# Layer 2's Wo on packed rows, one uncast Q/K product, quarter loads of x, and instruction orders as lists

## Chip, cores and metric

The kernel runs on one core of one Trainium2 chip. The metric is device time of one execution in microseconds (us). The core has TensorE (PE, with its weight loads shown apart as PEld), VectorE (DVE), ScalarE (ACT), GpSimd (POOL) and SyncE (SP). SP computes nothing here; it issues most DMAs, one after the other in the order of its list, and so is a queue of its own.

## The reference

Four layers run in turn on x of 2048 tokens by 448 features: attention (A), gated product (B), A, B, with the same weights each time. Every layer normalises its input and adds its result to x.

```python
x = A_x
x = x + _A_ref(_layernorm(x, axis=-1), A_wqkv, A_wo)
x = x + _B_ref(_layernorm(x, axis=-1), B_w_gate, B_w_up, B_w_down)
x = x + _A_ref(_layernorm(x, axis=-1), A_wqkv, A_wo)
x = x + _B_ref(_layernorm(x, axis=-1), B_w_gate, B_w_up, B_w_down)
```

A has 16 heads of 28 features. A token attends to itself and the seven tokens 2, 4, ... 14 back; the heads' outputs go through Wo (448 by 448). B computes (x Wgate) * (x Wup) with 1792 features, then Wdown.

## The kernel before

All of x and all weights stay on chip. The kernel calls the layers 0 to 3; layers 0 and 2 are A, layers 1 and 3 are B. A layer is cut into four chunks of 512 tokens, and `SEQ` (line 230) interleaves chunks of neighbouring layers: A00 A01 B10 A02 B11 and so on, where B12 is layer 1, chunk 2.

**Units.** `ln_chunk` (743) normalises four blocks of 128 tokens: statistics on DVE (`bn_stats`, 751), a logarithm and an exponential on ACT that give rstd (754, 756), the normalisation on DVE (772) and a transpose, either on PE with an eviction (781, 787) for the chunks that `PE_T` (30) names, or by a DMA that SP issues (775). `qk_chunk` (838) makes Q and K of a chunk in four units, each with a K and a Q half that run at the same time on the two halves of PE's 128 rows; a unit is two parts (`crossed`, 795), the second of which starts once the first has left PE. Evictions go to `qk` (872). `v_group` (887) makes V for a group of one or two query blocks of 120 tokens; there are 9 groups, g0 to g8. `attn_front` (940) makes logits (958), exponentials (970) and masks them (979); `attn_back` (1003) multiplies by V (997), sums, inverts on ACT (1026, 1027) and writes normalised heads to `oT` (1047). In layer 2 the logits of one group and the V product of the group before are one PE unit (`pe_joint`, 931). `y_blocks` (1052) does the Wo product for two neighbouring blocks of tokens, and `x_block` (1064) adds it to x. `b_chunk` (1075) makes 14 gate/up units of 128 features (1095), evicts (1101) and multiplies (1104) them, then runs the down product in four parts for each of two pairs of blocks (834).

**Padding.** In `oT` and `wo_g` a head has 32 rows, 28 of them used: four heads in 128 rows, four such chunks c for 16 heads. The Wo product of two blocks goes through these four chunks for each half of the rows, in two "flips", one for each pairing of row halves with blocks: 16 matmuls of 64 rows and 448 columns. The last four of 32 rows hold zeros in `wo_g`. Q and K of chunks 2 and 3 and of layer 2 already use such spare rows, filled by DMAs from `qk` to `qk` (878); chunks 0 and 1 of layer 0 (`FULLQ`) do not.

**Start.** SP and ACT load x's chunk 0 in two halves, then V's weights, then the Q/K weights into `stage`, which is the not yet used `hT`. ACT, DVE and GpSimd cast them into `WQK` with 32 rows for a head (lines 695 to 706, priority -28), 12 copies, and all Q/K units wait for all of them (`WQKR`). PE runs warm-up matmuls (692) until data is there. Gate/up weights are loaded in 14 steps, each behind the one before (713 to 716).

**Order.** `Sched` lays all units out before the program is emitted: it keeps a clock for every engine and takes the ready unit with the best priority. `TUNE` shifts priorities of single units by number. The outcome is one fixed list for each engine, which the engine runs strictly in order, waiting on semaphores where a unit's inputs come from elsewhere.

Of the kernel before, what the change touches and what calls it, by code (L numbers as in the profile page):

```python
# [29 lines left out]
PE_T = ("00","01","02")  # L30
# [8 lines left out]
POOL_MASK = 1  # L39
WQK_ENGS = ("act", "dve", "pool")  # L40
FULLQ = ("00", "01")
LN0 = (2,2)
# [4 lines left out]
TUNE = {  # L47
# [185 lines left out]
def qb_info(qb):  # L233

    if qb == 0:
        return 0, 128, 0, 128
    tok = 128 + QB * (qb - 1)
    return tok - 8, 128, tok, QB


STRADDLE = next(q for q in range(NQB) if qb_info(q)[2] < HALF < qb_info(q)[2] + qb_info(q)[3])
assert qb_info(STRADDLE)[0] + KW == HALF


def group_span(g):

# [30 lines left out]
class Sched:  # L277
# [34 lines left out]
    def finish_of(self, key):  # L312
        op, n = self.ready[key]
        if op.dma is not None:
            return max(o.end + o.lat for o in self.dgroup[(op.dma, op.mode)])
# [260 lines left out]
def build(nc, A_x, A_wqkv, A_wo, B_w_gate, B_w_up, B_w_down, out):  # L576
# [46 lines left out]
    def one(fn, key=None):  # L623
        return [(fn, key)]
# [630 lines left out]
```

## Time and profile before

| what | us |
|---|---|
| three runs | 395.64, 395.96, 396.29 |
| profiled execution, its own time | 395.34 |
| span of its profile | 393.5 |
| PE busy | 383.4 |
| DVE busy | 268.7 |
| ACT busy | 182.8 |

The granted clock is 1.00 in all stretches. The span begins with GpSimd's first constant and ends with the last store. PE's busy share contains 48 warm-up matmuls (8.9 us). Rows of the chain of waits show a start, a length and an engine with its line; "issue" is time in which the profile shows nothing that the engine waited for. Rows of stretches show start and end, length, busy time of each engine, the granted clock, the DMA share and GB/s.

### The profile page before, as it was taken

Reading aid. Unit: us, or ns where it says so; the run is one execution under the profiler, and the core shown is the slowest. Engines: PE = TensorE matmul, PEld = TensorE weight load, DVE = VectorE, ACT = ScalarE, POOL = GpSimd, SP = SyncE. Lnnn points to the kernel's source line nnn. Section 1 sums busy time; section 2 is a strip of 40 time slices with the busy share of each in tenths; the row PEclk is TensorE's granted clock in tenths of the full one; section 3 lists DMA queues with packets and bytes.
Section 4 is the critical chain, followed back from the end, with each engine's and each line's share of the span. In section 5 each row is a group of like instructions: output and inputs, shape, how many; then the busy total and the mean of one; then the engine's idle time right before and its main releaser. Section 6 shows DMA issues by size and latency. Waiting matters only on the chain.

```text
span 393.5 us, 12725 instructions
## 1 busy us (share of the span) xinstructions
PE 383.4 (97%) x5678; PEld 208.5 (53%) x5678; DVE 268.7 (68%) x577; ACT 182.8 (46%) x297; POOL 8.9 (2%) x29
## 2 busy tenths in 40 slices
PE   8999978999999999999999989999999999999997
PEld 6545544445545454455445545577545555544555
DVE  5996999997996375367874678843689893244323
ACT  4788775554536442464334543333646442134110
POOL 6110000000000000000000000000000000000000
DMA  8645473524230072000330002510003204100002
GB/s 273 189 91 132 109 110 105 85 49 50 48 42 15 13 97 55 2 13 4 66 68 16 16 3 50 72 28 13 27 26 72 27 2 93 45 5 2 23 2 72
DMA packets 50766, 21.74 MB, mean 55 GB/s; under 512 B 41912, under 2 KB 49816, under 8 KB 50712
## 3 DMA queue, kind: packets, MB, share of 16 engines
q1 hardware_dynamic: 49720, 19.95, 25.5%
q8 instruction: 45, 0.74, 0.8%
q10 hardware_dynamic: 992, 0.98, 0.7%
q14 instruction: 9, 0.07, 0.1%
HBM read 8.43 MB, written 1.84 MB: 26 GB/s over the span
## 4 chain that ended last, share of the span: by engine, by line
PE 92%; DVE 3%; DMA 2%; issue 1%; ACT 1%; ACTq 0%
PE ps L1095 43%; PE ps L834 26%; PE ps L818 16%; PE ps L958 2%; PE ps L997 2%; PE ps L1116 1%; DMA hT<-in_A_wqkv_dram 1%; DMA xnTb<-xn_sb 1%; DVE xn_sb L772 1%; DVE hT L1104 1%; ACT g_sb L1101 0%; ACTq L631 0%; DVE E_sb L979 0%; PE ps L781 0%; DVE qk L872 0%
## 5 line engine op out<-in xcount | busy, mean ns | idle before, releaser
L1095 PE MATMUL ps<-xnTb,WGU 64*128 64x512 bf16 x1568 | 178.4, 376 | 1.2 <-DMA xnTb<-xn_sb 0.9
L1095 PEld LDWEIGHTS ps<-xnTb,WGU 64*128 64x128 bf16 x1568 | 85.1, 94 | 84.5 <-issue 6.1
L1101 ACT ACTIVATE g_sb<-ps 128x512 bf16<-128x512 f32 x112 | 66.0, 596 | 110.2 <-PE ps L1095 86.4
L1104 DVE TENSOR_TENSOR hT<-g_sb,ps 128x512 bf16<-128x512 bf16 x112 | 75.8, 683 | 53.6 <-ACT g_sb L1101 50.6
L834 PE MATMUL ps<-WD,hT 64*128 64x448 bf16 x840 | 85.5, 349 | 0.1
L834 PEld LDWEIGHTS ps<-WD,hT 64*128 64x128 bf16 x840 | 43.9, 94 | 35.5 <-DVE hT L1104 0.6
L1065 DVE TENSOR_TENSOR x_sb<-x_sb,ps 128x448 bf16<-128x448 bf16 x62 | 35.8, 614 | 26.2 <-PE ps L834 26.2
L818 PE MATMUL ps<-xnTa,WQK 64*128 64x512 bf16 (+1 forms) x448 | 47.7, 356 | 0.0
L970 ACT ACTIVATE E_sb<-ps 128x1024 bf16<-128x1024 f32 (+1 forms) x36 | 33.6, 977 | 14.3 <-PE ps L958 13.9
L772 DVE TENSOR_SCALAR xn_sb<-x_sb,mv,rstd 128x512 bf16<-128x512 bf16 (+1 forms) x64 | 35.5, 581 | 6.2 <-ACT rstd L756 6.1
L751 DVE BATCH_NORM_STATS2 st<-x_sb 128x6 f32<-128x448 bf16 x64 | 37.4, 611 | 2.3 <-DMA x_sb<-in_A_x_dram 2.3
L818 PEld LDWEIGHTS ps<-xnTa,WQK 64*128 64x128 bf16 x448 | 23.5, 94 | 19.4 <-DVE qk L872 0.5
L834 PE MATMUL ps<-wo_g,oT 64*128 64x448 bf16 x256 | 30.5, 350 | 1.5 <-issue 1.5
L818 PE MATMUL ps<-WV,xnTa 64*128 64x448 bf16 (+1 forms) x252 | 28.5, 340 | 0.7 <-DVE hT L1104 0.4
L872 ACT ACTIVATE qk<-ps 128x1024 bf16<-128x1024 f32 (+1 forms) x23 | 21.5, 948 | 14.0 <-PE ps L818 13.9
L754 ACT ACTIVATE lnv<-mv,eps_sb 128x2 f32<-128x2 f32 x32 | 9.5, 300 | 32.7 <-DVE mv L753 32.7
L979 DVE TENSOR_TENSOR E_sb<-E_sb,MK 128x1024 bf16<-128x1024 bf16 (+2 forms) x39 | 23.2, 610 | 1.3 <-ACT E_sb L970 1.2
L1047 DVE TENSOR_TENSOR oT<-ps,R_sb 128x448 bf16<-128x448 f32 (+2 forms) x38 | 21.0, 597 | 2.8 <-ACT R_sb L1027 2.7
L1026 ACT ACTIVATE R_sb<-R_sb 128x960 f32<-128x960 f32 (+1 forms) x18 | 17.3, 961 | 11.4 <-DVE R_sb L1024 11.4
L872 DVE CAST qk<-ps 128x1024 bf16<-128x1024 f32 (+1 forms) x9 | 9.9, 1102 | 16.1 <-PE ps L818 16.1
L834 PEld LDWEIGHTS ps<-wo_g,oT 64*128 64x128 bf16 x256 | 12.6, 94 | 12.8 <-issue 1.9
L818 PEld LDWEIGHTS ps<-WV,xnTa 64*128 64x128 bf16 x252 | 12.2, 94 | 10.8 <-PE ps L818 1.6
(45 smaller groups left out, 179.2 us busy)
## 6 DMA issues: line engine op xcount, KB each, us to landing
out_dram<-x_sb SPq DMA_DIRECT2D x15, 112.0 KB, 1.7
WGU<-in_B_w_gate_dram SPq DMA_DIRECT2D x7, 224.0 KB, 3.4
WGU<-in_B_w_up_dram SPq DMA_DIRECT2D x7, 224.0 KB, 3.7
WD<-in_B_w_down_dram SPq DMA_DIRECT2D x14, 112.0 KB, 2.1
x_sb<-in_A_x_dram SPq DMA_DIRECT2D x3, 448.0 KB, 7.1
qk<-qk SPq DMA_DIRECT2D x24, 28.0 KB
xnTb<-xn_sb SPq DMA_TRANSPOSE x32, 3.1
hT<-in_A_wqkv_dram SPq DMA_DIRECT2D x2, 224.0 KB, 5.2
```

Of the source, the lines that this page charges most:

```text
L751: sc.add("dve", one(lambda E, B=B: E.bn_stats(st6[:, B, :], x_sb[:, B, :]), ("bn", li, B)), 525.0, deps=[("x", li - 1, B)] + ([("xn", li - ...
L772: sc.add("dve", one(lambda E, B=B, dst=dst, src=src: E.tensor_scalar(dst, src, mv[:, B, 0:1], rstd[:, B:B + 1], ALU.subtract, ALU.mult), ( ...
L818: parts[0 if s < 3 else 1][1].append((lambda E, w=w, c=c, lo=lo, st=st, sp_=sp_: E.matmul(u["out"](w), u["lhs"](w, c, lo, lo + 64), u["rhs ...
L834: ins.append((lambda E, w=w, c=c, lo=lo, st=st, sp_=sp_: E.matmul(outs(w), lhs(w, c, lo), rhs(w, c, lo), start=st, stop=sp_), keys[w] if s ...
L872: return E.activation(dst, src, ACT.Copy) if hasattr(E, "activation") else E.tensor_copy(dst, src)
L970: return E.activation(E_sb[:, slot, 2 * hp:2 * hp + 2, 0:w], ps[:, b0:b0 + 2, 0:w], ACT.Exp, scale=SCALE)
L979: return E.tensor_tensor(e, e, m, ALU.mult)
L1047: return E.tensor_tensor(dst, src, rec, ALU.mult)
L1065: sc.add("dve", one(lambda E: E.tensor_tensor(x_sb[:, B, :], x_sb[:, B, :], ps[:, bk[w], 0:D], ALU.add), ("x", li, B)), dve_est(D), deps=[ ...
L1095: ins.append((lambda E, u=u, k=k, w=w: E.matmul(u["out"](w), WGU[64 * w:64 * w + 64, k, 128 * u["fc"]:128 * u["fc"] + 128], X[64 * w:64 * ...
L1101: sc.add("act", one(lambda E, gs=gs, bk=bk: E.activation(g_sb[:, gs, 0:n], ps[:, bk[0], 0:n], ACT.Copy), ("G", li, jp, fc)), act_est(n), d ...
L1104: sc.add("dve", one(lambda E, gs=gs, bk=bk, fc=fc: E.tensor_tensor(hT[:, fc, hs, h0:h1], g_sb[:, gs, 0:n], ps[:, bk[1], 0:n], ALU.mult), ( ...
```

## The change

1. **Layer 2's Wo.** The 16 heads have 448 features and need only 7 half chunks of 64 rows for each block, not 8. For all chunks of layer 2 (`WX`), `move_heads` sends heads 12 to 15 of two blocks, 8 small loads for each chunk of tokens, from chunk 3 of `oT` to spare rows: two heads for one of the blocks, the other two for the other. `wo_g` gets three more slots with the other two heads' rows: a copy of slots 0 to 2 on ACT or DVE (`wo_c`) and 10 small loads behind layer 0's Wo. `y_twin` replaces `y_blocks`: it pairs blocks B and B+2 and runs 8 matmuls in the first flip and 6 in the second, and waits for all 8 loads of the chunk.
2. **One uncast Q/K product.** The first unit of layer 0, chunk 0 (`DIRECT`) reads `stage` itself: 56 matmuls of 64 rows by 32 columns of weights, four side by side for each that was, instead of 14.
3. **Weight casts** go to ACT and DVE alone, behind the normalisation of block 3.
4. **x's chunk 0** comes in four loads, two on SP and two on ACT.
5. **Transposes** of layer 0's chunk 2 go by DMA instead of PE (`PE_T`).
6. **Small moves:** zeroing `wo_g` goes from DVE to GpSimd, the mask of chunk 0 from GpSimd to DVE; some reuse waits name all readers instead of the last.
7. **Orders.** `TUNE` is empty; `ORDER` gives the list of units of every engine by number, and the clock's picture of loads and of PE's instruction loads is extended (it now only chooses PSUM banks, since the order is given).

```diff
-PE_T = ("00","01","02")
+PE_T = ("00", "01")
...
-POOL_MASK = 1
-WQK_ENGS = ("act", "dve", "pool")
+POOL_MASK = 0
+WQK_ENGS = ("act", "dve")
+WQK_P = -18.6
 FULLQ = ("00", "01")
+DIRECT = ("000",)
+BULK = "sp"
+CHAIN = True
+WX_ENG = "sp"
+WX = ("20", "21", "22", "23")
...
-TUNE = {
...
+TUNE = {}
+ORDER = {
+    "pe": [
...
+WX_MOVES = (((0, 64, 4), (2, 80, 3), (1, 96, 4), (3, 112, 3)),
+            ((2, 0, 4), (0, 16, 3), (3, 32, 4), (1, 48, 3)))
...
+                if ORDER:
+                    op = self.ops[ORDER[e][len(order[e])]] if len(order[e]) < len(ORDER[e]) else None
+                    if op is None or op not in pend[e] or self.ready_at(op, e) > now + 1e-6:
+                        continue
...
-    load_x(0, (0, 1, 2), "sp", 2400.0, -60)
-    load_x(0, (1, 2, 2), "act", 3000.0, -60)
...
+    load_x(0, (0, 1, 4), "sp", 2150.0, -60)
+    load_x(0, (1, 2, 4), "act", 2300.0, -60)
+    load_x(0, (2, 3, 4), "sp", 2170.0, -59.9)
+    load_x(0, (3, 4, 4), "act", 2400.0, -59.9)
...
-    memset("dve", wo_g[:], 0.0, "c_wo", 1000)
+    memset("pool", wo_g[:, 0:4, :], 0.0, "c_wo", 1400)
...
-            sc.add(WQK_ENGS, one(fn, ("wqk", c, w)), dict(zip(("act", "dve", "pool"), ests)), deps=[("stg", c), "c_wqk0"], prio=-28)
+            sc.add(WQK_ENGS, one(fn, ("wqk", c, w)), dict(zip(("act", "dve", "pool"), ests)), deps=[("stg", c), ("xn", 0, 3), "c_wqk0"], prio=WQK_P)
...
+        def fw(E):
+            return E.activation(wo_g[:, 4:7, :], wo_g[:, 0:3, :], ACT.Copy) if hasattr(E, "activation") else E.tensor_copy(wo_g[:, 4:7, :], wo_g[:, 0:3, :])
+        sc.add(("act", "dve"), one(fw, "wo_c"), {"act": 1350.0, "dve": 800.0}, deps=WO, prio=-17.5)
...
+                        plain_dma("sp", wo_g[pads, s:s + z - a, :], rows[:, a:z, :], ("wop", o, b, a), "d_wop", deps=plain + ["wo_c"], lat=1600.0, prio=-16.5, svc=(300.0, 700.0))
...
+                for b in range(u.get("cols", 0)):
+                    ins.append((lambda E, w=w, c=c, lo=lo, st=st, sp_=sp_, b=b: E.matmul(
+                        u["out"](w)[32 * b:32 * b + 32], u["lhs"](w, c, lo, lo + 64)[b], u["rhs"](w, c, lo, lo + 64), start=st, stop=sp_, tile_position=(lo, 32 * b)),
+                        u["keys"][w] if sp_ and b == 3 else None))
...
+            direct = f"{li}{j}{c}" in DIRECT
...
+                if direct:
+                    o = 2 * D * dc + (0 if which else D) + 4 * DH * c
+                    return [stage[lo:hi, o + DH * b:o + DH * b + 32] for b in range(4)]
...
+    def move_heads(li, j, o, prio):
+        t0 = 512 * j % HALF + 256 * o
+        B = 4 * j + 2 * o
+        nd = [("N", li, g) for g in range(NGRP) if group_span(g)[2] < 128 * (B + 2) and group_span(g)[3] > 128 * B]
+        for b, row, m in WX_MOVES[o]:
+            plain_dma(WX_ENG, oT[32 * b + DH:32 * b + 32, 0:m, t0:t0 + 256], oT[row:row + 4 * m, 3, t0:t0 + 256], ("WX", li, j, o, b), f"d_w{o}{j}", deps=nd,
+                      lat=2000.0, prio=prio - 0.3, mode=li, est=680.0 if WX_ENG == "sp" else 500.0, svc=(300.0, 700.0))
+
+    def y_twin(li, B, prio):
+        bk = Banks(2, pair=BPAIR)
+        j = B // 4
+        cols = (128 * (B % 8), 128 * ((B + 2) % 8))
+        keys = (("Y", li, B), ("Y", li, B + 2))
+        parts = []
+        for flip in (0, 1):
+            ins = []
+            for c in range(3 if flip else 4):
+                for h in (0, 1):
+                    w, lo = h ^ flip, 64 * h
+                    ins.append((lambda E, w=w, c=c, lo=lo, flip=flip: E.matmul(ps[:, bk[w], 0:D], oT[lo:lo + 64, c, cols[w]:cols[w] + 128], wo_g[lo:lo + 64, c + 4 if w and c < 3 else c, :],
+                                                                             start=flip == 0 and c == 0, stop=flip == 1 and c == 2), keys[w] if flip and c == 2 else None))
+            parts.append((flip, ins, []))
+        crossed(parts, [("WX", li, j, o, b) for o in range(2) for b in range(4)] + WOP, prio, pe_cols(D), bk)
+        for w in range(2):
+            x_block(li, B + 2 * w, bk, w, keys[w], prio)
...
+                    if f"{li}{B // 4}" not in WX:
+                        y_blocks(li, B, pr)
+                        continue
+                    move_heads(li, B // 4, B // 2 % 2, pr)
+                    if B % 4 == 2:
+                        y_twin(li, B - 2, pr)
+                        y_twin(li, B - 1, pr)
```

The numbers in `ORDER` count the calls that add a unit. Read with that count, the lists say this of the places that matter below. PE: four transposes, the two V units of g0 and g1, the uncast Q/K unit, the other three units of chunk 0, four transposes of chunk 1, the logits of g0 and g1, Q/K of chunk 1, V of g3 and g2, logits of g2, Wo of blocks 0 and 1, Q/K of chunk 2. In layer 2, between the joint unit of g3 and g2 and the first Wo part of chunk 0 there stand three gate/up units and five down parts; between the V product of g8 and the first Wo part of chunk 3 two down parts, the Wo of chunk 2 (two pairs of blocks), one gate/up unit and four down parts. ACT: the copy `wo_c` stands behind the first Q/K eviction and ahead of the second. SP: the four transposes of chunk 2 stand among gate/up loads 2 and 3.

More of the change, by code (lines that the diff above doesn't have):

```diff
@@ L261 @@
     __slots__ = ("engs", "ins", "est", "deps", "mode", "prio", "acquire", "release", "idx", "eng",
-                 "dma", "lat", "after", "start", "end", "seen", "selfd")
+                 "dma", "lat", "svc", "land", "after", "start", "end", "seen", "selfd")
     def __init__(self, **kw):
@@ L314, in finish_of @@
         if op.dma is not None:
-            return max(o.end + o.lat for o in self.dgroup[(op.dma, op.mode)])
+            return max(o.land for o in self.dgroup[(op.dma, op.mode)])
         if n == len(op.ins) - 1:
@@ L357, in pick_banks, with fetch_delay, landing @@
         return cand[:req.n]
+    def fetch_delay(self, now, est, n):
+        a, self.fetched = self.fetched, self.fetched + n
+        z, late = self.fetched, 0.0
+        k = int((a - self.NEED) // 256) + 1
+        while k >= 0 and 256 * k + self.NEED < z:
+            if k in self.arrive and 256 * k + self.NEED >= a:
+                late = max(late, self.arrive[k] - (now + late + est * (256 * k + self.NEED - a) / n))
+            k += 1
+        k = max(0, int((a - self.ASK) // 256) + 1)
+        while 256 * k + self.ASK < z:
+            if k not in self.arrive:
+                ask = now + late + est * max(0.0, 256 * k + self.ASK - a) / n
+                self.arrive[k] = max(ask + self.FETCH, self.arrive.get(k - 1, 0.0) + 1300.0)
+            k += 1
+        return late
+    def landing(self, op):
+        if op.svc is None:
+            return op.end + op.lat
+        svc, tail = op.svc
+        a = max(op.end + op.lat - tail - svc, self.moving)
+        z = a + svc
+        for k in sorted(self.arrive):
+            f1 = self.arrive[k]
+            f0 = f1 - self.FETCH_DMA
+            if f0 < z and f1 > a:
+                z += f1 - max(a, f0)
+        self.moving = z
+        return z + tail
     def schedule(self):
+        self.fetched, self.arrive, self.moving = 0, {}, 0.0
         self.ready_cache = {}
@@ L394, in schedule @@
                 best = None
+                if ORDER:
+                    op = self.ops[ORDER[e][len(order[e])]] if len(order[e]) < len(ORDER[e]) else None
+                    if op is None or op not in pend[e] or self.ready_at(op, e) > now + 1e-6:
+                        continue
+                    if op.acquire is not None and self.pick_banks(op.acquire, now) is None:
+                        continue
+                    best = op
                 cands = []
-                for op in pend[e]:
+                for op in () if ORDER else pend[e]:
                     r = self.ready_at(op, e)
@@ L460, in schedule @@
                     mode = op.mode
+                    est += self.fetch_delay(now, est, 2 * len(op.ins))
                 op.start, op.end = now, now + est
+                op.land = self.landing(op)
                 free[e] = op.end
@@ L497, in schedule @@
         self.order = order
-        self.total = max(op.end + op.lat for op in self.ops)
+        self.total = max(op.land for op in self.ops)
     def emit(self, nc, block, sems):
@@ L800, in crossed @@
                 xid[0] += 1
-                tags = [("cross", xid[0], h) for h in (0, 1)]
-                ins = ins[:-2] + [(fn, [t] + ([k] if k is not None else [])) for (fn, k), t in zip(ins[-2:], tags)]
+                tags = [("cross", xid[0], h) for h in range(2 * cols)]
+                ins = ins[:-2 * cols] + [(fn, [t] + ([k] if k is not None else [])) for (fn, k), t in zip(ins[-2 * cols:], tags)]
                 nextk = tags
@@ L861, in rhs @@
                 return X[lo:hi, dc, t0:t0 + n]
[L862 removed]
+            return dict(bk=bk, out=out, lhs=lhs, rhs=rhs, n=n, deps=[("stg", k) for k in range(4)] + ["c_stg"] if direct else WQKR, keys=(("Kps", li, j, c), ("Qps", li, j, c)), c=c, **({"cols": 4} if direct else {}))
         us = [unit(c) for c in range(4)]
```

106 lines of the change are left out of this document (66 added, 40 removed), and 226 rows, old and new, of tables (ORDER, TUNE).

## The prediction

> **What bounds the kernel now.** I read the page first, then the chain of work that ended last, then busy times by stretch, then single tiles. The page has TensorE at 97% of the span; the second row is the instruction queue, used below.
>
> ```profile
> PE 383.4 (97%) x5678; PEld 208.5 (53%) x5678; DVE 268.7 (68%) x577; ACT 182.8 (46%) x297; POOL 8.9 (2%) x29
> ...
> q8 instruction: 45, 0.74, 0.8%
> ```
>
> That share counts warm-up matmuls too, so I cut the span where the first real product starts (about 11.2 us) and where the first gate/up product starts (60.8 us). In the busy times by stretch the first number is the length, then PE, its weight loads, DVE, ACT, POOL:
>
> ```profile
> 11.18:18.60 7.42, 7.42 (x78) 3.56 (x78) 6.70 (x22) 4.81 (x13) 0.00 (x0) 1.00 0.62 160
> 18.60:22.20 3.60, 3.29 (x76) 2.35 (x76) 3.57 (x9) 3.55 (x8) 0.00 (x0) 1.00 0.49 126
> 22.20:34.50 12.30, 12.21 (x317) 6.01 (x318) 10.77 (x31) 10.52 (x18) 1.27 (x1) 1.00 0.52 100
> 34.50:60.80 26.30, 23.00 (x584) 12.49 (x583) 23.33 (x54) 20.97 (x26) 0.00 (x0) 1.00 0.56 116
> 60.80:391.20 330.40, 327.99 (x4572) 177.30 (x4572) 217.06 (x447) 137.73 (x226) 0.00 (x0) 1.00 0.21 38
> ```
>
> Three regimes: before 11.2 us no useful product at all; from there to 60.8 PE idles 0.31 + 0.09 + 3.30 = 3.7 us, with DVE nearly full (23.33 of 26.30); after 60.8 PE idles only 330.40 - 327.99 = 2.4 us. So after 60.8 time falls only by PE work taken out or by those 2.4 us; ahead of it, by an earlier start or less idling. The chain in order of time (start, length, what) has the prices:
>
> ```profile
> 11.26 7.43 PE ps L818 x76
> ...
> 22.24 2.26 PE ps L818 x20
> ...
> 56.46 4.07 DMA xnTb<-xn_sb
> 60.53 0.25 issue
> 60.77 1.69 PE ps L1095 x14
> ...
> 100.94 1.51 PE ps L1095 x14
> 102.46 1.32 PE ps L834 x14
> 103.78 0.61 PE ps L997 x64
> 104.39 0.86 PE ps L834 x8
> ...
> 184.78 0.61 PE ps L997 x64
> ...
> 231.80 0.61 PE ps L997 x64
> 232.41 0.72 PE ps L834 x5
> 233.13 1.46 issue
> ```
>
> A pair of matmuls on the two row halves costs 1.51 / 7 = 0.216 us at 512 columns and 1.32 / 7 = 0.189 us at 448. Behind attention products the Wo half unit took 0.86 us where 4 x 0.189 = 0.76 was due: 0.10 us to change tile shape. And 1.46 of the 2.4 us is one hole in the middle of a Wo half unit (5 of its 8 matmuls before it), with no engine to blame.
>
> **Layer 2's Wo: -1.5 us.** A pair of blocks needs 8 pairs of matmuls now (4 chunks, two flips), 7 afterwards. Layer 2 has 8 pairs of blocks: 8 x 0.189 = 1.5 us of PE work, in the stretch where PE is full. It comes out whole unless PE waits in its place.
>
> **The price of the moves: +0.3 us.** Each of four chunks now needs 8 small SBUF-to-SBUF loads on SP behind the normalised heads (N), and the product waits for all of them. 32 such loads and 10 of spare weight rows join the SP queue. The nearest rows are the present head moves (issue: min/median/max ns) and a plain load of 112 KB (last number, us to landing):
>
> ```profile
> L631 SPq DMA_DIRECT2D qk<-qk x8: 627/638/791, 41.8 to 53.5; - x8
> ```
> ```profile
> WD<-in_B_w_down_dram SPq DMA_DIRECT2D x14, 112.0 KB, 2.1
> ```
>
> What lies between the attention product and N has these ends, read with the chain's 184.78 and 231.80 (timeline of DVE, start and length):
>
> ```profile
> 189.92 1.22 DVE L1047 TENSOR_TENSOR oT<-ps,R_sb 128x448 bf16<-128x448 f32 x2
> ```
> ```profile
> 239.20 1.27 DVE L1047 TENSOR_TENSOR oT<-ps,R_sb 128x448 bf16<-128x448 f32 x3
> ```
>
> 185.39 to 191.14 is 5.75 us; 232.41 to 240.47 is 8.1 us. Add four issues of 0.64 (2.6) and a landing of 2.1 less the issue, 1.5: 9.8 to 12.2 us. The PE list puts this between the joint attention product and the first Wo part of chunk 0: 3 gate/up units and 5 down parts, 3 x 1.51 + 5 x 1.32 = 11.1 us. Chunk 3 has one gate/up unit, six down parts and chunk 2's Wo (two pairs of blocks, 14 pairs of matmuls): 1.51 + 6 x 1.32 + 14 x 0.189 = 12.1 us, though its moves queue behind chunk 2's. Chunks 1 and 2 have more. So the two tight places cost between nothing and about 1.1 + 0.1 us; the list keeps few vector instructions between attention and N there, as in the short chain, so I take 0.3. PE takes its list in order, so everything behind the product waits too: that is why it counts in full. Vector's adds and layer 3's statistics behind it have chunks of slack. On SP, layer 3's transposes queue behind the moves, at most 8 x 0.64 = 5 us, again under gate/up units of the other chunk; if that cover failed, PE would lose those 5 us.
>
> **The start: a lead of 1.8 us.** The timeline of DVE for the first normalisation:
>
> ```profile
> 4.34 1.15 DVE L751 BATCH_NORM_STATS2 st<-x_sb 128x6 f32<-128x448 bf16 x2 [2.33 <-DMA x_sb<-in_A_x_dram]
> ...
> 6.81 0.70 DVE L772 TENSOR_SCALAR xn_sb<-x_sb,mv,rstd 128x512 bf16<-128x512 bf16 x2
> 7.43 0.27 DVE L705 COPY WQK<-hT 128x448 bf16<-128x448 bf16 x1
> 8.60 1.54 DVE L772 TENSOR_SCALAR xn_sb<-x_sb,mv,rstd 128x512 bf16<-128x512 bf16 x2 [0.90 <-ACT rstd L756]
> ```
> ```profile
> L705 POOL COPY WQK<-hT x6: 555/622/1100, 7.6 to 10.5; 128x448 bf16<-128x448 bf16 x4, 128x112 bf16<-128x112 bf16 x2
> L705 ACT ACTIVATE WQK<-hT x5: 560/567/706, 7.6 to 11.1; 128x448 bf16<-128x448 bf16 x3, 128x112 bf16<-128x112 bf16 x2
> ```
>
> The second pair of blocks waits 0.90 us for rstd, which sits behind weight casts on ACT, and then takes 1.54 instead of 0.70 us while GpSimd copies weights. Afterwards the casts depend on block 3's normalisation and GpSimd makes none: the pair can end at 7.51 + 0.70 = 8.2 instead of 10.14, 1.9 us earlier. Four quarter loads instead of two halves let the first statistics start up to 0.7 us earlier (half the bytes of a load that now lands around 4.3) or not at all, since bytes and queues are the same; I take 0.4. So real products start at about 8.9.
>
> Then the casts come due. Behind its three evictions of transposes (at most 0.6 each) ACT has six casts, 6 x 0.57 = 3.4 us, from about 7.8: done at 13.1. PE meanwhile has both first V units (7 pairs of 224 and 7 of 448 columns, 7 x 0.095 + 7 x 0.189 = 2.0 us) and the uncast Q/K product. That product is 56 matmuls on 64x32 tiles where 14 were. No such tile with 512 columns is in the trace. The nearest row is L997: 64 products of 64x32 tiles with 64 columns in 0.61 us, 9.5 ns each, which would take 64 x 0.027 = 1.7 us one after another; so at least 2.8 run at once. All 8 at once gives 7 x 0.216 = 1.5 us plus 0.10; 2.8 at once gives 4.3. The row's 9.5 ns may be issue alone, and 8 issues fit into 0.216 us, so I take 1.6: PE is ready at 12.5 and waits 0.6 for casts. The remaining three Q/K units, 4.5 us, end at 17.7. Before, the same point (Q/K done at 18.69, with 8 matmuls, 0.76, of the second V unit still due) is 19.45: a lead of 1.8 us.
>
> From there to 60.8 I keep 1.8, between two ends. Chunk 2's transposes leave PE:
>
> ```profile
> 18.50:22.30 3.80, 2.29 (x32) 1.81 (x32) 1.00 0.50 133
> ```
> ```profile
> DMA to landing us min/median/max: 2.4/3.6/5.2
> ```
>
> The first row is two chunks of transposes on PE, so one is 1.15 us, with four evictions besides. In their place four DMA transposes go on SP among the gate/up weight loads; the second row is what such transposes took at 24 to 36 us in that company. Q/K of chunk 2 began at about 34.5 us with its data long there. Afterwards the DVE list has 30 instructions from the last Q/K eviction of chunk 0 (17.8) to the last normalisation of chunk 2; at the 31 in 12.30 us of the stretch above that is 11.9 us, so the transposes land at 29.7 + 2.4 to 29.7 + 5.2, 32.1 to 34.9, against a PE ready at 34.5 - 1.8 = 32.7. Also new there: a copy of 3 x 448 columns on ACT, at most 3 x 0.567 = 1.7 us, ahead of Q/K evictions, and one mask moved from GpSimd to DVE. Against that stand 1.15 us less of PE work and the 3.30 us idle ahead of 60.8, of which the list may save some. Ends: from +0.4 (transposes 2.2 late, the lead of 1.8 gone) to -5.5 (lead plus all 3.7 idle). The first cost and the first savings are of like size, which leaves the lead. Zeroing Wo moves from DVE, which waits 2.33 us for x there anyway, to GpSimd: nothing, as Wo is first used only behind layer 0's first attention groups.
>
> **The order lists: -0.7 us.** PE issued 5678 + 5678 instructions, and the instruction queue moved 45 blocks: one per 252. The hole at 233.13 follows 128 attention products, 256 instructions in 1.3 us, so I read it as a late block. Another list moves products against block borders: it is gone (-1.46) or elsewhere (0). I take half.
> [...]
>
> **Sum**, against the profiled run's own 395.34 us (span 393.5 and 1.8 around it): -1.5 + 0.3 - 1.8 - 0.7 = -3.7, so 391.6. The median shown, 395.96, is 0.6 above the profiled run: 392.3.
>
> **Rivals.**
> The lead is swallowed (0.18): the first gate/up product waits for a DMA transpose (56.46, 4.07 us), which hangs on DVE's order, and DVE is full ahead of it. For: 23.33 of 26.30. Against: DVE's work, too, starts earlier. 392.3 + 1.8 = 394.1.
> The lists also close most of the idle time ahead of 60.8 (0.15): 2.5 of 3.7 gives 389.8. For: those waits are of order (DVE ran masks between two normalisations that the transposes needed). Against: DVE has little room.
> The hole at 233 isn't a late block, or comes back elsewhere (0.10): 392.3 + 0.7 = 393.0. [...]
> The uncast product isn't what it says: its column tiles run only 2.8 at once (0.05): +2.7, 395.0.
> Slower: moved heads land late (0.10). Place: the first Wo part of chunks 0 and 3. With the long 8.1 us, 2.6 of issue and a landing of 3.6 (median of the transposes above) the chain is 14.3 us against 11.1 and 12.1 covered: 3.2 + 2.2 = 5.4 us, less the 0.3 in the sum, 397.4. It decides once both waits together pass 4 us. Against: the DMA share is 0.21 after 60.8, where it was 0.56 around those transposes.
>
> **How the numbers follow.** My forecast has 0.42, the rivals as above. A measurement of this kernel tells 0.2%, 0.8 us, from no change: faster means under 395.2. Forecast, swallowed lead, closed idle and the hole lie under it (0.85), the column tiles at its edge, late moves above; with some blur 0.81 faster, 0.07 the same, 0.12 slower. The range takes in the closed-idle case with 0.5 to spare (389.3), and on the other side the column tiles, and a lost lead with chunk 2's transposes 2.2 us late on top (394.1 + 2.2 = 396.3); it leaves out most of the late moves.
>
> **What would show it.** Right: real products from about 9 us; DVE's second pair of blocks at 0.35 each; no wait between the uncast product and the next Q/K unit over 1 us; first gate/up at about 59; 240 Wo matmuls in place of 256; no hole of 1.4 us inside a unit. Wrong: a PE wait on a DMA ahead of the first Wo part of chunk 0 or 3, Q/K of chunk 2 waiting for transposes past 36 us, or an uncast product of 4 us.

## The result, and the profile after

| | median us | runs | ratio to before, 95% interval |
|---|---|---|---|
| before, same chip | 395.80 | 395.43 to 396.29 | |
| after | 398.73 | 398.44 to 399.51 | 1.0076, 1.0058 to 1.0095 |

Slower by 2.9 us, where 3.7 us less was forecast. The profiled execution took 398.59 us, its span 396.8 at a mean granted clock of 0.996 (before 393.5 at 1.000).

First the page of the changed kernel, then its busy times by stretch. The first two stretches begin at the first real product (9.70) and at the first gate/up product (57.48); the third is a piece in the middle of the span that stands out.

```profile
PE 385.2 (97%) x5688; PEld 201.8 (51%) x5688; DVE 264.9 (67%) x579; ACT 183.6 (46%) x298; POOL 6.0 (2%) x24
...
q8 instruction: 45, 0.74, 0.8%
```
```profile
9.70:57.48 47.78, 45.68 (x1065) 23.42 (x1066) 41.79 (x113) 41.34 (x64) 0.00 (x0) 1.00 0.74 144
57.48:177.60 120.12, 119.41 (x1884) 62.31 (x1880) 89.47 (x192) 59.03 (x98) 0.00 (x0) 1.00 0.27 49
177.60:184.40 6.80, 3.92 (x54) 1.62 (x54) 2.42 (x8) 2.23 (x3) 0.00 (x0) 0.75 0.06 14
184.40:286.90 102.50, 102.34 (x1344) 53.25 (x1340) 64.80 (x133) 41.98 (x72) 0.00 (x0) 1.00 0.19 33
286.90:394.20 107.30, 105.03 (x1291) 54.68 (x1290) 60.68 (x118) 35.48 (x58) 0.00 (x0) 1.00 0.16 35
```

In these rows PE is as full as before (97%), and the first gate/up product comes 3.3 us earlier (57.5 against 60.8). The loss lies behind it: 2.88 us idle and a granted clock of 0.75 in 6.8 us, and 2.27 us idle in the last stretch. The chain of waits (start, length, what) has the places:

```profile
56.30 0.46 issue
...
177.35 0.27 PE ps L969 x32
177.62 2.88 issue
180.50 0.32 PE ps L969 x32
180.82 3.08 PE ps L1093 x14
...
285.88 1.05 PE ps L803 x10
286.93 0.96 issue
287.90 1.88 PE ps L803 x18
...
303.13 1.24 PE ps L1093 x9
304.37 1.00 issue
305.37 0.80 PE ps L1093 x5
```

The rows of "issue" shown here are four holes (idle stretches of PE inside a unit), 5.30 us, with no engine to blame, like the one of before. The 2.88 splits an attention product after 32 of its 64 matmuls. And the gate/up unit behind it took 3.08 us where 14 such matmuls took 1.51 us before: another 1.57 us.

To set this against the whole, I gave each matmul from the first V product on its step in the undisturbed stream (0.108 us for 512 columns on a row half, 0.0946 for 448, and so on) and summed; "other" is the rest, waits, holes and slow clock:

| us | before | after |
|---|---|---|
| first V product starts | 11.2 | 9.7 |
| matmuls at their steady step | 366.9 | 365.0 |
| other | 12.7 | 19.5 |
| behind the last matmul | 2.6 | 2.6 |
| span | 393.5 | 396.8 |

The start gave 1.5 us and the work 1.9, as the change says; "other" took 6.8 back. The 5.30 us of holes and 1.57 of slow matmuls make 6.9, less the hole of 1.46 that the kernel before had: 5.4. The remaining 1.4 of the 6.8 are waits of other kinds.

### The profile page after: what moved, and what is told of

Read it like the earlier page. It is cut to its first block, busy times and chain, and to the rows that moved or that the text cites. A ratio compares the mean times of both kernels' runs of the same rounds, so it can differ in the third digit from the quotient of the medians.

```text
span 396.8 us, 12781 instructions
## 1 busy us (share of the span) xinstructions
PE 385.2 (97%) x5688; PEld 201.8 (51%) x5688; DVE 264.9 (67%) x579; ACT 183.6 (46%) x298; POOL 6.0 (2%) x24
## 4 chain that ended last, share of the span: by engine, by line
PE 87%; ACT 4%; DVE 3%; issue 3%; DMA 2%; SPq 1%; DVEq 0%
PE ps L1093 41%; PE ps L803 21%; PE ps L783 14%; PE ps L1055 3%; PE ps L930 3%; PE ps L969 2%; PE ps L639 2%; PE ps L1114 1%; DMA xnTb<-xn_sb 1%; DMA qk<-qk 1%; DVE hT L1102 1%; ACT R_sb L999 1%; ACT R_sb L998 1%; ACT qk L844 1%; DVE xn_sb L735 1%
## 5 line engine op out<-in xcount | busy, mean ns | idle before, releaser
L1093 PE MATMUL ps<-xnTb,WGU 64*128 64x512 bf16 x1568 | 180.5, 378 | 1.6 <-issue 1.0
L1093 PEld LDWEIGHTS ps<-xnTb,WGU 64*128 64x128 bf16 x1568 | 82.2, 94 | 88.5 <-issue 8.6
L1099 ACT ACTIVATE g_sb<-ps 128x512 bf16<-128x512 f32 x112 | 64.7, 595 | 124.4 <-PE ps L1093 121.9
L1102 DVE TENSOR_TENSOR hT<-g_sb,ps 128x512 bf16<-128x512 bf16 x112 | 74.7, 683 | 66.7 <-ACT g_sb L1099 64.5
L803 PEld LDWEIGHTS ps<-WD,hT 64*128 64x128 bf16 x840 | 41.7, 94 | 39.2 <-issue 2.4
L783 PE MATMUL ps<-xnTa,WQK 64*128 64x512 bf16 (+1 forms) x434 | 45.2, 356 | 0.0
L783 PEld LDWEIGHTS ps<-xnTa,WQK 64*128 64x128 bf16 x434 | 21.8, 94 | 20.1 <-DVE hT L1102 0.9
L998 ACT ACTIVATE R_sb<-R_sb 128x960 f32<-128x960 f32 (+1 forms) x18 | 17.3, 959 | 7.3 <-DVE R_sb L996 3.9
L999 ACT ACTIVATE R_sb<-R_sb 128x960 f32<-128x960 f32 (+1 forms) x18 | 17.3, 958 | 0.3
L969 PE MATMUL ps<-E_sb,v_sb 64*32 64x64 bf16 (+1 forms) x1088 | 12.0, 195 | 3.3 <-issue 3.3
L897 ACT ACTIVATE v_sb<-ps 128x896 bf16<-128x896 f32 x14 | 12.7, 913 | 4.6 <-PE ps L783 4.6
```

Of the source, the lines that this page charges most:

```text
L783: ins.append((lambda E, w=w, c=c, lo=lo, st=st, sp_=sp_: E.matmul(u["out"](w), u["lhs"](w, c, lo, lo + 64), u["rhs"](w, c, lo, lo + 64), s ...
L803: ins.append((lambda E, w=w, c=c, lo=lo, st=st, sp_=sp_: E.matmul(outs(w), lhs(w, c, lo), rhs(w, c, lo), start=st, stop=sp_), keys[w] if s ...
L998: sc.add("act", one(lambda E: E.activation(flat, flat, ACT.Ln), ("Rl", li, g)), act_est(4 * n * nr, False), deps=[("Rs", li, g, 0), ("Rs", ...
L1093: ins.append((lambda E, u=u, k=k, w=w: E.matmul(u["out"](w), WGU[64 * w:64 * w + 64, k, 128 * u["fc"]:128 * u["fc"] + 128], X[64 * w:64 * ...
L1099: sc.add("act", one(lambda E, gs=gs, bk=bk: E.activation(g_sb[:, gs, 0:n], ps[:, bk[0], 0:n], ACT.Copy), ("G", li, jp, fc)), act_est(n), d ...
L1102: sc.add("dve", one(lambda E, gs=gs, bk=bk, fc=fc: E.tensor_tensor(hT[:, fc, hs, h0:h1], g_sb[:, gs, 0:n], ps[:, bk[1], 0:n], ALU.mult), ( ...
```

## The experiments

**Theory A:** a hole comes where TensorE's instruction stream crosses from one block of 256 instructions into the next before that one has arrived. What decides is how the block borders fall against the stretches that use instructions fastest, so the change moved the holes by moving instruction numbers. **Theory B:** the moved heads, the loads or the new order of work make the holes.

The trace bears A out first. Counted over all records of PE's queue, each of the four holes begins at a record whose number leaves 193 when divided by 256 (2241, 6081, 8897, 9665), and the one of before does too (7617). These records are weight loads, matmuls and semaphore waits, in order of time. In the changed kernel there are 11510 of them and 45 packets of 16 KB in the instruction queue, one for 256. The packets around the holes, us:

```
border passed   packet             next border reached   work resumed
169.12          170.12 to 171.29   172.94                at once
172.94          178.24 to 179.11   177.44                180.50
180.50          181.85 to 182.94   191.53                at once
284.61          285.52 to 286.44   286.58                287.90
287.90          289.02 to 290.15   294.69                at once
301.72          302.82 to 303.97   303.99                305.37
```

In the fourth and sixth rows the packet starts 0.9 to 1.1 us behind the border and takes about 1, and work goes on 1.4 us after its end: 3.3 to 3.7 us from border to use, as if only one block were held ahead. (Elsewhere a packet can start ahead of the border, as at 118.24 for the border at 118.84: the times are those at which work passed it.) An attention unit (64 logits and 64 attention products, 256 instructions) takes 1.3 us. The second row is worse: its packet started 5.3 us behind the border, only when the next one was reached.

**Shifts alone.** Small matmuls ahead of the warm-up move every border by two instructions each; half as many warm-up matmuls are shortened to make room. No other work changes, though the first V product came up to 1.5 us earlier or later. The kernel before gets 9 and 48 of them, the changed one 46 and 22.

```diff
+PADS = 9
+SHORT = 4
+WARM_COLS = 128
...
-        sc.add("pe", one(lambda E: E.matmul(ps[:, wb[0], 0:256], warm[:, 0:128], warm[:], start=True, stop=True), ("warm", n)), 214.0 ...
+        pads = [(lambda E, b=b % 4: E.matmul(ps[32 * b:32 * b + 32, wb[0], 0:64], warm[0:64, 0:32], warm[0:64, 0:64], start=True, stop=True, tile_position=(0, 32 * b)), None)
+                for b in range(PADS if n == 0 else 0)]
+        wc = WARM_COLS if n < SHORT else 256
+        sc.add("pe", pads + one(lambda E, wc=wc: E.matmul(ps[:, wb[0], 0:wc], warm[:, 0:128], warm[:, 0:wc], start=True, stop=True), ("warm", n)), 214.0 ...
```

> The kernel before with 9 small matmuls more among the warm-up matmuls (18 PE instructions, two for each), so that every border between blocks of 256 instructions comes 18 instructions earlier in the program; warm-up shortened by about as much. Theory A (holes in PE's work are late instruction blocks, set by where a border falls against the bursts of 256 attention instructions): the hole of 1.46 at 233 us goes and at most 0.3 comes up elsewhere: 395.8 - 1.3 = 394.5. Theory B (holes come of waits, orders and DMA traffic, borders play no part): 395.8, hole at 233 as before.

> The kernel before with 48 small warm-up matmuls more (96 PE instructions). Theory A: holes of about 2.1 at 51, 1.7 at 172, 0.8 at 187 and 1.7 at 282 us in place of the one at 233: 395.8 + 4 = 399.8, more if a hole of 2 us brings the clock down. Theory B: 395.8.

> The changed kernel, same lists, with 46 small warm-up matmuls more (92 PE instructions). Theory A: the holes at 177 (2.88), 287 (0.96), 304 (1.00) and 56 us (0.46) go, and with the first the stretch of half clock behind it (1.5); one of 0.8 comes at 95 us: 398.7 - 5.9 = 392.8. Theory B (moved heads and the new order make the holes): 398.7 within 0.5.

> The changed kernel with 22 small warm-up matmuls more (44 PE instructions). Theory A: the holes move: 0.7 at 38, 0.9 at 96, 1.8 at 170, 2.1 at 226, 0.8 at 282 us, 6.7 in all, about what the changed kernel has now: 398 to 400, but at these places, and none at 177 or 304. Theory B: 398.7 with the holes where they are.

| kernel | instructions added | median us | ratio, interval | holes in the chain, start and length | clock |
|---|---|---|---|---|---|
| before | 0 | 395.7 | | 233.13 1.46 | 1.000 |
| before | 18 | 394.95 | 0.9973, 0.9956 to 0.999 | 300.73 0.47 | 1.000 |
| before | 96 | 399.59 | 1.0089, 1.0068 to 1.011 | 53.53 0.52, 58.35 1.53, 176.65 1.69 | 0.996 |
| changed | 92 | 395.33 | 0.9993, 0.9977 to 1.001 | 296.90 2.63 | 0.991 |
| changed | 44 | 404.5 | 1.0205, 1.018 to 1.023 | 37.32 0.46, 171.19 1.61, 228.67 1.42, 286.37 2.67, 306.97 2.33 | 0.987 |

The same lists with the same moves give 395.3 to 404.5, and the kernel before 394.95 to 399.6: B can't make that. The holes of each kernel go, others come. Two forecasts of the time missed: 46 left one hole of 2.63 us I had not foreseen, and 22 made larger ones, one at 307 us where none was forecast. With 48 the time came out (399.8 forecast) by luck in part: of its four places, those at 187 and 282 us came to next to nothing, and the hole at 58 us was not foreseen. The chain of the changed kernel with 46, and its PE row by single us (length, busy and matmuls, granted clock):

```profile
296.68 0.23 PE ps L975 x28
296.90 2.63 issue
299.53 0.51 PE ps L975 x32
300.05 2.24 PE ps L1099 x9
```
```profile
298.00:299.00 1.00, 0.00 (x0) 0.92 0.11 22
299.00:300.00 1.00, 0.47 (x38) 0.50 0.35 119
300.00:301.00 1.00, 1.00 (x9) 0.50 0.04 9
```

Here too the packet started 5.0 us behind its border, and the clock halved behind the hole: 8 or 9 gate/up matmuls touch a microsecond at 0.50, 12 to 14 one at 1.00.

**Time or number?** In the next kernel the start alone moves: the first 12 warm-up matmuls have 128 columns, nothing is added, each instruction keeps its number.

```diff
+PADS = 0
+SHORT = 12
```

> The changed kernel with the first 12 warm-up matmuls shortened to 128 columns and nothing added: everything after the warm-up begins about 1.5 us earlier, every instruction keeps its number. Theory A (the place of a border in the instruction stream decides): the long holes come at the same instructions as in the changed kernel, so about 1.5 us earlier by the clock (near 54.8, 176.1, 285.4, 302.9), in about the same sizes, 2.88 and about 1 and 1 among them; time 397.2 (396.3 to 398.3). Theory D (a hole comes from what else is under way at that moment, a transfer or another engine's fetch that happens to fall together with it): with the start moved alone the holes change places or sizes freely; the 2.88 one goes with a chance of a half, 394 to 398.

Measured 399.34 us, 1.0085 (1.0057 to 1.0113). Long holes at the same four records, 2241, 6081, 8897, 9665: 0.86, 2.60, 1.65 and 1.00 us in the chain. The number decides, as theory A has it. Its time did not come out (396.3 to 398.3 was forecast), nor did the holes move earlier: the first V product came 1.4 us earlier, yet the first gate/up at 57.9, so nothing of it came through. The longest hole splits the same attention product behind the same 32 matmuls (L975 here is L969 in the changed kernel):

```profile
178.17 0.27 PE ps L975 x32
178.44 2.60 issue
181.04 0.32 PE ps L975 x32
```

**Borders placed.** If A is right, borders can be put where the stream is slow. From the trace with 46 I counted for each shift how closely two borders follow each other in each stretch. No single shift serves all, so the borders are moved again on the way: some gate/up matmuls of 512 columns are cut into two of 256, which adds four instructions for each pair at the same work.

```diff
+SPLIT = {(1, 3): 24, (3, 0): 54}
+PADS = 66
+SHORT = 31
...
+                cuts = ((0, n // 2), (n // 2, n)) if k and FC * (k - 1) + m < SPLIT.get((li, j), 0) else ((0, n),)
+                for s0, s1 in cuts:
+                    for w in range(2):
+                        ins.append((lambda E, u=u, k=k, w=w, s0=s0, s1=s1: E.matmul(u["out"](w)[:, s0:s1], WGU[64 * w:64 * w + 64, k, 128 * u["fc"]:128 * u["fc"] + 128],
...
```

> The changed kernel with its block borders placed: 66 small matmuls ahead of the warm-up (132 instructions more from there on; the first 31 warm-up matmuls shortened to 128 columns make room), 24 pairs of gate/up matmuls of layer 1's last chunk cut into two halves of 256 columns (96 more instructions from about 219 us), and 54 pairs of layer 3's first chunk (216 more from about 259 us). Theory A (a hole comes where the PE passes two block borders, 256 instructions apart, in less than about 3.5 us): with these places no two borders stand under 3.9 us apart anywhere in the order of the changed kernel, so no hole over 0.5 us is left, no stretch of low clock follows, and the first V at 8.2 us (as in the run with 46) holds; the sum is first V 8.2 + steady work 365.0 + some 11.5 of other waits + 2.6 behind the last matmul + about 0.3 for the cuts = span 387.6, time 389.4 (388.5 to 391.5). Theory B (the moved heads and the new order lists make the holes, the instruction count is chance): the lists and the moves are as in the changed kernel, so holes of 5 to 7 us in all stay: 395 to 398.5. Theory C (the slower clock comes from the change itself, not from the holes): clock 0.996 or less and 391.5 to 393 even without holes.

Measured 392.19 us (390.64 to 392.54), ratio 0.9895 (0.9871 to 0.9918), clock 1.000, no hole left at a border. B, with 395 us or more, is out; C, which had the slow clock come of the change itself, is out by the clock of 1.000. Theory A's holes are gone, but the time is 2.8 us above its 389.4 and outside its range. The first V product came at 8.7, and by the same sum of steps the other waits until 30 us were 3.9 us against 1.9 in the changed kernel: a start moved forward seems to be eaten at once. So next the same with 13 shortened instead of 31, and from it two parts of the change undone one at a time: the uncast product, and layer 2's Wo.

```diff
-DIRECT = ("000",)
+DIRECT = ()
```
```diff
-            for c in range(3 if flip else 4):
+            for c in range(4):
...
-... start=flip == 0 and c == 0, stop=flip == 1 and c == 2), keys[w] if flip and c == 2 else None))
+... start=flip == 0 and c == 0, stop=flip == 1 and c == 3), keys[w] if flip and c == 3 else None))
```

> The run with placed borders (66 small matmuls ahead, cuts 24 and 54) with only the first 13 warm-up matmuls shortened, so that the first V starts where it starts in the changed kernel (about 9.7 us and not 8.7). Theory E (an earlier start is eaten by waits on the loads and casts before 30 us): the first V a microsecond later costs nothing, the first gate/up stays at 57.3 to 57.9, the other waits until 30 us fall from 3.9 to about 2, time 392.0 (391.0 to 392.6). Theory F (a microsecond at the start is a microsecond at the end): 393.2 (392.7 to 394). Both expect no hole at a border and a clock of 1.000.

> The run before this one with the uncast product undone: the list of products on uncast weights is empty, so chunk 0's first Q/K product is 14 matmuls on the cast weights at its old place in the order, and waits there for all casts; 42 more small matmuls ahead (22 warm-up matmuls shortened) keep the borders where they are. If the uncast product carries the lead at the start, the TensorE waits 2 to 3 us more before 20 us, the first gate/up comes at 59.5 to 60.5 and the time is 2 to 2.5 us above that run: 394 to 394.5. If the lead is eaten by waits in front of the first gate/up anyway: the same time within 0.6, 391.5 to 392.6.

> The run with placed borders and the first 13 shortened, with layer 2's Wo back to 16 matmuls for a pair of blocks: the second half of each pair's product also runs over the fourth 128-row group, so that the heads in it are counted twice in layer 2 (the output is not the reference's); moves, loads and lists stay; the cuts fall to 22 and 52, so that the borders keep their places. If the 16 matmuls that the change removed lie on the path in full: 16 by 0.0946 us = 1.5 us slower than that run, 393.5 (393.0 to 394.1). If they lie beside a wait in layer 2: less than 0.5 slower.

| kernel, borders placed | median us | ratio, interval |
|---|---|---|
| 13 shortened | 391.67 (391.23 to 393.54) | 0.9889, 0.9858 to 0.992 |
| and uncast product undone | 392.10 (391.64 to 393.36) | 0.9898, 0.9871 to 0.9925 |
| and Wo's 16 matmuls back | 393.50 (391.85 to 395.73) | 0.9926, 0.9902 to 0.9949 |

The third counts the heads of chunk 3 twice in layer 2. The first beats both kernels. Its first V product came at 8.8 us all the same, so by itself it can't decide between E and F. The other runs speak for E: with 12 shortened the first V at 8.3 gave a first gate/up at 57.9, and in the kernel with the copy moved, below, 9.6 gave 57.0. At the place of the 2.88 us hole its chain has the same work in one piece and the gate/up unit behind it at the full clock:

```profile
176.75 0.70 PE ps L937 x64
177.46 0.72 PE ps L976 x64
178.18 1.62 PE ps L1102 x14
```

Wo's matmuls cost 1.8 us by the medians and 0.37% or 1.5 us by the ratios, as forecast if they lie on the path in full. (The execution whose trace was kept is the fastest of twelve, 391.85 us, and its span is no longer than the other's, so this rests on the medians.) The uncast product is worth 0.4 us by the medians, inside the spread of the runs, not the 2 to 2.5 it would be if it carried the lead. With it, the chain at the start runs through Wo's load and its copy on ACT; without it, through the weights' load and their casts, and PE reached the first gate/up only 0.6 us later (57.8 against 57.2). The two chains, with it and without:

```profile
9.23 7.09 DMA wo_g<-in_A_wo_dram
16.32 0.02 issue
16.34 1.32 ACT wo_g L672
17.66 1.83 ACT qk L851 x2
```
```profile
3.19 7.64 DMA hT<-in_A_wqkv_dram
...
11.06 1.82 ACT WQK L659 x3
```

**Is it the copy, then?** One number moved in ACT's list puts the copy behind 67 us.

```diff
-        1, 3, 4, 6, 8, 10, 15, 145, 146, 151, 152, 158, 161, 164, 88, 89, 94, 95, 93, 90, 246, 237, 169, 175, 170, 176, 102, 238, 240, 182, 179, 188,
+        1, 3, 4, 6, 8, 10, 15, 145, 146, 151, 152, 158, 161, 164, 88, 89, 94, 95, 93, 90, 246, 237, 169, 175, 170,  176, 238, 240, 182, 179, 188,
...
-        559, 560, 368, 371, 469, ...
+        559, 560, 368, 371, 102, 469, ...
```

> The run with placed borders and the first 13 shortened, with one number moved in ScalarE's list: the copy of Wo's spare rows (op 102) stands behind a gate copy of layer 1's first chunk (about 67 us) and no longer ahead of the second Q/K eviction. In that run ScalarE waits 1.56 us for Wo's load and copies for 1.32 us there, with two evictions and three transposes' evictions behind it. Theory J (the change's own copy eats the lead at the start): evictions of Q/K follow at 14.8 us, the first gate/up product comes at 54.5 to 56.2 (57.2 there), time 390.2 (389.3 to 391.0), ratio to before 0.985. Theory K (VectorE or the head moves bound the stretch before the first gate/up): first gate/up within 0.5 of 57.2, time 391.7 (391.1 to 392.6), ratio 0.989.

Measured 391.50 us (390.44 to 391.99), ratio 0.9883 (0.9848 to 0.9917), first gate/up at 57.0: not the copy, as theory K has it. Which of K's two, VectorE or the head moves, bounds that stretch was not set apart. ACT (its timeline) now stands idle for PE where it waited and copied before:

```profile
15.23 0.33 ACT L726 ACTIVATE rstd<-lnv 128x2 f32<-128x2 f32 x2
16.82 1.94 ACT L851 ACTIVATE qk<-ps 128x1024 bf16<-128x1024 f32 x2 [1.26 <-PE ps L790]
```

**The kernel before with placed borders.** 9 small matmuls ahead and 33 pairs cut in layer 3's first chunk.

```diff
+SPLIT = {(3, 0): 33}
+PADS = 9
+SHORT = 4
```

> The kernel before with its block borders placed too: 9 small matmuls ahead (18 instructions, as in the first run), and 33 pairs of gate/up matmuls of layer 3's first chunk cut into halves of 256 columns (132 more instructions before about 255 us). Theory A: the 1.5 us hole at 233 is gone as with 9, and so is the 0.84 us one at 300 that remained: 0.4 to 0.8 below that run, 394.3 (393.8 to 395.0). Set beside the changed kernel with placed borders (391.67) it gives what the change is worth by itself: 2.6 us less. If the cuts cost what the hole gives back, 394.9 and no gain over the run with 9.

Measured 394.55 us (394.15 to 396.22, and one execution of 400.13), ratio 0.995 (0.9926 to 0.9975), no hole at a border. That is the footing for the change, with the borders out of the way in both: 391.67 against 394.55 us, 2.9 us less by the medians, which come from two chips, and 2.4 us less by the ratios, 0.9889 against 0.995.

**The clock.** Does it halve because PE stands still? Four waits in layer 3's last gate/up products, away from any border:

```diff
+STALL = {(3, 2, 2): 2, (3, 2, 9): 4, (3, 3, 0): 1, (3, 3, 13): 5}
+HELD = {(3, 2, 7): 2, (3, 2, 13): 9, (3, 3, 3): 0, (3, 3, 7): 13}
...
+            held = [("H", li, jp, HELD[li, j, m])] if (li, j, m) in HELD else []
+            sc.add("pe", ins, 7 * pe_cols(n), deps=u["deps"] + tdeps + held, mode=MAIN, prio=prio, acquire=u["bk"])
...
+                    more.append((lambda E, gs=gs, bk=bk, c=c, s=s: E.tensor_tensor(WQK[:, c, 4 * s:4 * s + 4, :].rearrange("p s e -> p (s e)"), g_sb[:, gs, 0:n], ps[:, bk[1], 0:n], ALU.mult), None))
+                sc.add("dve", more + [(mul, ("H", li, jp, fc))], dve_est(n),
```

> The run with placed borders and the first 13 shortened, with four waits put into layer 3's last two gate/up products, far from any border: at four places the next unit waits for the gate-times-up product of the unit ahead of it, which takes 0.6 us on ScalarE and 1, 2, 4 or 5 times 0.69 us on VectorE (the extra times write into the Q/K weights, which nobody reads any more). Holes of about 1.6, 2.3, 3.7 and 4.4 us, 12 in all, with nothing late in the fetch. Theory G (the clock falls because TensorE stood still): behind the holes of 2.3 us and more the steps double from about 0.108 to about 0.21 us for some 3 us, as behind the 2.88 us hole of the changed kernel, 1.5 us lost each; behind 1.6 nothing; time 391.7 + 12 + 4.5 = 408 (406.5 to 409.5), clock under 0.99. Theory H (the clock falls for another cause that goes with the late blocks or with the changed kernel): steps at full rate behind all four, clock 1.000, 403.7 (402.5 to 405).

Measured 407.76 us, clock 0.987: theory G, but for the wait of 2.37 us, behind which it had the clock fall too. From the last matmul's start to the next PE stood for 2.37, 3.56, 1.79 and 4.16 us. Rows of single microseconds behind the first two and the fourth:

```profile
338.00:339.00 1.00, 0.24 (x4) 1.00 0.51 9
339.00:340.00 1.00, 1.00 (x12) 1.00 0.89 184
...
346.00:347.00 1.00, 0.00 (x0) 1.00 0.00 0
347.00:348.00 1.00, 0.00 (x0) 0.58 0.00 0
348.00:349.00 1.00, 0.68 (x4) 0.50 0.00 0
...
353.00:354.00 1.00, 1.00 (x8) 0.51 0.00 0
354.00:355.00 1.00, 1.00 (x14) 1.00 0.08 16
...
374.00:375.00 1.00, 0.44 (x4) 0.73 0.00 0
375.00:376.00 1.00, 1.00 (x8) 0.50 0.00 0
...
377.00:378.00 1.00, 1.00 (x8) 0.56 0.00 0
```

Behind 2.37 and 1.79 the clock stays; behind 3.56 it is half for 6.8 us, from 347.2 until 354.0, and behind 4.16 for 3.4 us, from 374.5 to 377.9 (a microsecond at 0.58 has 0.84 us of it at half). So a half clock behind a long hole can be the hole's consequence alone and needs nothing of the change.

## Why the prediction was wrong

**The order lists, -0.7: the step that failed.** The mechanism was named rightly, "I read it as a late block", and so was its trigger, "another list moves products against block borders". Wrong was the bound: "it is gone (-1.46) or elsewhere (0)". It counted the one hole that the old order happened to have and took that as the most a new order could have. The changed order has nine attention units of 128 products, each holding a border somewhere and so nine chances of a second border within 3.5 us (from border to use it was 3.3 to 3.7 above); the old one had eleven. The lists as given met four, 5.30 us, and the halved clock added 1.57. The holes of the changed kernel are of two sizes: 0.46 to 1.00 us where the packet started at most 1.1 us behind its border, and 2.88 where it started 5.3 us behind. The term came out near +5.4 (6.9 less 1.46), and no rival held it: the third allowed the old hole to stay or come back once.

In all the holes at borders, in seven kernels, work went on 1.3 to 1.6 us behind the end of a packet that had started only behind the border before, as if PE held no more than the block at work and the next. That is my reading of these times; how much PE holds was not shown otherwise. The distance of two borders alone doesn't make a hole: with 9 on the kernel before, borders at 230.88 and 232.62 us were both passed at once, and there the packet had started ahead of the first, at 229.50.

**Layer 2's Wo, -1.5:** right. 240 matmuls in place of 256, and 1.5 to 1.8 us measured by putting them back.

```profile
L803 PE MATMUL ps<-wo_g,oT 64*128 64x448 bf16 x128 | 14.4, 350 | 0.5 <-DVE oT L1019 0.3
L1055 PE MATMUL ps<-wo_g,oT 64*128 64x448 bf16 x112 | 11.3, 349 | 0.0
```

**The price of the moves, +0.3:** nothing. The second row above has 0.0 us idle ahead of layer 2's products, so no moved head was late there and the slower rival fell at its named place. The kernel was slower for another reason.

**The start, -1.8:** mis-sized at both ends. The second pair of blocks takes 0.35 us each, as said (four in 1.42, timeline of DVE):

```profile
3.34 1.68 DVE L714 BATCH_NORM_STATS2 st<-x_sb 128x6 f32<-128x448 bf16 x3 [2.26 <-DMA x_sb<-in_A_x_dram]
...
5.81 1.42 DVE L735 TENSOR_SCALAR xn_sb<-x_sb,mv,rstd 128x512 bf16<-128x512 bf16 x4
```

But the first product came at 9.70, not 8.9: the warm-up matmuls, made for the later x, held PE until 7.8 us (with 12 of them shortened it came at 8.3). At the first gate/up the lead was 3.3 us, since the idle time ahead of it shrank too, from 3.7 to 2.1 us, as the second rival had it. At the end only about 1 us of it is left: 2.9 less Wo's 1.8 by the medians, 2.4 less 1.5 by the ratios. That the lead was not the uncast product's doing, nor the start's, is shown by the runs: undoing the one cost 0.4 us, moving the other nothing. Which of the rest (the four loads, the casts on two engines, the order) made it wasn't tried.

**The uncast product:** "all 8 at once" was right. In the trace the starts of eight matmuls follow those of the eight before at 0.216 us, the step of one pair; between the first 24 and the other 32 another 0.45 us passed. 56 matmuls took 2.10 us, with no wait behind them for the next unit:

```profile
11.87 1.00 PE ps L786 x24
12.87 0.04 issue
12.92 1.06 PE ps L786 x32
13.97 4.64 PE ps L783 x42
```

So 2.1 instead of 1.6 us, far from the 4.3 of one end. **Chunk 2's transposes** were not late: its Q/K product began at 34.4 us, where 36 was the mark.

**The sum without the lists' term** was -1.5 + 0.3 - 1.8 = -3.0. With placed borders in both kernels the difference is -2.9 by the medians and -2.4 by the ratios. The close match is luck in part: the lead at the first gate/up was 1.5 us larger than the sum had it, and some 2 us that it had not were lost behind it.

**Open:** why some packets started so late. In the changed kernel the DMA share was 0.03 (7 GB/s) in the 5.30 us from the border at 172.94 to its packet. Five started 3.1 to 5.3 us behind their border, 0.3 to 0.8 us after work had reached the next one: at 178.24 in the changed kernel, at 178.61 with 12 shortened, at 296.97 with 46, at 286.63 and 307.05 with 22. Their holes are the five longest, 2.33 to 2.88 us in the chain. At the first and third the border came 3.82 and 3.55 us behind the one before; with 46 another came 3.58 us behind (169.63) and its packet was in time. It wasn't tried. Nor were the waits behind the first gate/up followed up: from there to the last matmul the placed kernel takes 330.2 us (57.2 to 387.4) and the kernel before with placed borders 328.8 (62.0 to 390.8), though layer 2's Wo is 1.5 us less.

## What to carry to other kernels

Where a stream has stretches of hundreds of instructions in little over a microsecond (here 256 in 1.3 us), find the block borders by counting, and price any edit that adds, removes or reorders instructions by all the places where two borders could come close, not by the hole that today's order shows: the same kernel ran from 391.7 to 404.5 us by that alone. Before an order is judged slow, shift it by a few instructions and look whether its holes move. Cutting matmuls in halves in a quiet stretch moves borders at little cost: in the placed kernel a pair cut in two took 0.218 us where a whole one takes 0.216, about 0.2 us for all 78.

## What the runs showed of the hardware

An idle stretch need not be long to cost twice: the one of 2.88 us in the changed kernel had another 1.57 us lost behind it. In the run with four waits the clock halved behind 3.56 and 4.16 us and not behind 2.37. Holes at borders that were shorter than 3.56 us halved it too: 2.88 us in the changed kernel, 2.63 with 46, and 1.61 us (changed kernel with 22 small matmuls, where the clock was 0.50 from 174 to 177 us and the gate/up pairs behind the hole at 171 us took 0.42 us each), when an attention unit with its small tiles stood just ahead. But a hole of 1.42 us in the same run (228.67) and one of 1.65 with 12 shortened (287.32), with an attention unit 0.3 and 1.1 us ahead against 0.7 there, left the clock at 1.00. So neither the length of a hole nor the unit ahead of it decides alone.

The half clock lasted 6.8 us behind the wait of 3.56 us and 3.4 behind that of 4.16, and 3.4 behind the hole of 2.88 us in the changed kernel (0.75 granted over 6.8 us). What sets these lengths, and why one short hole halves the clock and another doesn't, no run here isolates.
